# A fused S4 convolution and S2-MLP gate on one core: a new instruction order, a shorter phase step, a second staging buffer for w3 and w4, and output stores from two engines

## The chip, the core and the metric

The kernel runs on one core of one Trainium2 chip. The metric is the time of one execution on the device in microseconds (us); every time given for a kernel is the median of several executions. TensorE (PE) does matrix products and transposes, VectorE (DVE) and ScalarE (ACT) do elementwise work out of SBUF and PSUM, SyncE (SP) issues DMA transfers. Each engine runs its own list of instructions strictly in order and waits on semaphores for the others.

## The reference

The input u is 2048 rows (positions) of 512 channels. It is layer-normed to xn, which goes down two branches whose results are multiplied:

```python
xn = _layernorm(x)
s = _A_ref(xn, ...)            # S4 convolution
g = _silu(_B_ref(xn, ...))     # S2-MLP
return x + s * g

# _A_ref, per channel d with 128 states n
P = exp(dt * A * l)                        # complex, l = 0 .. 2047
K = einsum("dn,dnl,dn->dl", C, P, dt * B).real
y = irfft(rfft(xn padded) * rfft(K padded))[:2048] + xn * Dskip

# _B_ref
h  = gelu(layernorm(xn) @ w1)              # 512 x 512
hs = concat(quarters of h shifted by +1, -1, +2, -2 rows) @ w2
x1 = xn + hs
return x1 + gelu(layernorm(x1) @ w3) @ w4  # 512 x 1376, 1376 x 512
```

## The kernel before, in words

**Recorded, then ordered.** The body of `tile_mixer_kernel` (L613) does not issue instructions. Every call on an engine is recorded as an `Op` in a `Plan` (L295) with its engine, a cost, its dependences, and for ACT the function table that it needs. `Plan.order` (L406) is a list scheduler: it always takes the engine that can start earliest and, among the ops that are ready on it, the one with the lowest due value. The due values are a table of numbers, `DUE`, one for each op. `SWITCH` is added to the due value of an ACT op that needs another function table than the loaded one. Some ops (copies, affine maps, shifts) may run on ACT or on DVE (`Either`, L577); `PREFER`/`AVOID` are added to their value on the one and on the other engine. Where PE is planned to wait long, it gets "filler" matmuls of the identity into an unused bank. `Plan.issue` (L478) then emits the instructions: line L484 emits every table load, L486 every filler, L487 everything else. So nearly all rows of the profile read L487, and the names of the tiles tell the steps apart.

**The steps, in program order.** `loads` and `params` read u (into X, 128 x 16 x 512, kept in SBUF) and the state parameters, which are transposed into `par`. `token_mixing` (L1355) does the first layer norm, h = gelu(.. @ w1) (`hT`, f32 matmuls `pb<-xT,w`), writes the first stage of the Fourier transform of xn to DRAM (`u_stage1`, tiles `ue`), adds the shifted h @ w2 to X (`hs_pair`, four pairs of `pd<-w,hT` matmuls and two adds `X<-X,pd` for a group of 256 rows, the "residual stage" below), and prepares w3 and w4: `weight_squares` squares them on ACT to get a common scale, then `prep` (L1183, six calls) loads one piece of w3 and one of w4 into the staging tile `wst`, and splits each into an f16 high and low part (`w3h`, `w4h`: one affine map on ACT or DVE and one subtraction on DVE). The place of `wst` holds one piece at a time.

`tables(hf)` (L973) builds K for half hf of the channels in 8 chunks of 32 channels: `block` (L863, one for two chunks) makes the coarse phases `pab` and magnitudes (`EB`, `mag`: many small Exp on ACT), `phases` adds the coarse phases, rounds the sum (`kt<-pt`, by adding and taking away a large constant), `remainders` subtracts, `waves` takes sine and cosine on ACT, `factors` and `sums` multiply on DVE by `eg` and `mag` in seven passes over 128 x 1024, and 64 small PE matmuls for a chunk (`pc<-pt`, `pc<-kt`; 128 records in the trace) reduce over the states into `kev`, which is stored to DRAM.

`u_spectra` (L1034) does the second Fourier stage of xn for half 1 in 8 units: `uin` and `cst` are loaded, 8 matmuls `pd<-uin,cst` (16 records), two copies to `uh`, a store. `kstage1(hf)` and `products(hf)` do the same for K, multiply the spectra (`pr`) and store the inverse's first stage (`z1e`, to the DRAM scratch Zda or Zdb).

`mlp_input(g)` and `mlp(g)` (L1298, L1313) are the MLP for a group g of 256 rows: layer norm to `x1n`, a transpose, a high part (a cast) and a low part (a subtraction) `x1T`, 132 up matmuls `pb<-x1T,w3h` (f16, three products for each block, 24 for a step, 12 in the last), gelu, `ghl`, 66 down matmuls `pa<-w4h,ghl`, and two `X<-pa,wsc,X` that add the result to X. Groups go in the order `GROUPS = [1, 2, 3, 4, 5, 6, 7, 0]` (L1296).

The end: `gate(g)` puts silu on X for group g. `inverse(hf, g)` loads `zin` (scratch Zda or Zdb), does 8 small matmuls into pc or pd, and multiplies X by them (two `X<-X,pd`). `finish(g)` adds u again (`X<-X,xr`) and stores to the output in four pieces.

**What sets the order.** SP issues all DMAs in the order that the scheduler wrote, so a load that waits for its buffer holds back all the later ones. There are eight PSUM banks, in pairs a, b, c and d: `pa` takes the MLP's accumulators (and `u_stage1`), `pb` the up products, transposes and h, `pc` the K reductions, `pd` the residual stage, transposes and `u_spectra`.

The shared staging buffer and the end of the program, before:

```python
wst = Ring(early + 2 * K4, K4, 1)                     # one place
...
for g in range(8):
    gate(g)
for hf in range(2):
    for g in range(8):
        inverse(hf, g)
for g in range(8):
    finish(g)
```

Of the kernel before, what the change touches and what calls it, by code (L numbers as in the profile page):

```python
# [10 lines left out]
F32 = mybir.dt.float32  # L11
# [8 lines left out]
P = 128  # L20
# [65 lines left out]
class Op:  # L86
# [22 lines left out]
KGC = 0.93  # L109
WARM = 36  # L110
QUARTERS = 1.05

DUE = (
# [150 lines left out]
)  # L264
SWITCH = 6.17
PREFERP, AVOIDP = 3.68, -2.58
# [1173 lines left out]
```

## Time and profile before

| | us |
|---|---|
| median of 3 runs | 597.78 (596.45 to 598.2) |
| the profiled execution | 597.6 |
| its span in the trace | 595.7 |
| PE busy | 554.6 (93%) |
| DVE busy | 503.5 (85%) |
| ACT busy | 452.4 (76%) |

The profiled execution took 597.6 us on the device, of which the trace's span is 595.7; its mean granted TensorE clock was 0.959. A group in the profile is named by line, engine, operation and output <- input tiles, with the shape of both; "x" is a count. Windows give the busy time of each engine in a stretch of the span, with the granted clock (PEclk, 1.00 is full speed) and the mean busy share of the 16 DMA engines. Waits give what ended an engine's idle time. SPq and PEq are the instruction queues of SP and PE.

### The profile page before, as it was taken

The page shows a single profiled execution, that of the slowest core. Times are in us where ns is not written, and L with a number is a line of the kernel's source. Part 1 is how long each engine was busy: PE and PEld are TensorE (multiplying, and loading weights), DVE is VectorE, ACT ScalarE, POOL GpSimd, SP SyncE. Part 2 cuts the span into 40 slices and gives each one's busy share as a digit, 9 for nine tenths or more (in the row PEclk, how much of TensorE's full clock was granted, in tenths as well). Part 3 has the DMA queues.
Part 4 walks back from the last instruction along what each step waited for, and adds up shares of the span by engine and source line. Part 5 has one row for each costly group of instructions (what it writes and reads, how often), then busy time and mean ns, then how long its engine had stood idle before and what let it go on. Part 6 is the DMA issues. An engine that isn't in the chain of part 4 may idle for free.

```text
span 595.7 us, 13857 instructions
## 1 busy us (share of the span) xinstructions
PE 554.6 (93%) x5560; PEld 355.0 (60%) x5560; DVE 503.5 (85%) x816; ACT 452.4 (76%) x959; POOL 0.7 (0%) x6
## 2 busy tenths in 40 slices
PE   9879979999958799999999999999999999999962
PEld 9766647644426466556566665666755666766410
DVE  6999999999997999999999999999965256557376
ACT  3799999999998599999999999999965452113300
POOL 0000000000000000000000000000000000000000
PEclk9979989999978799999999999999999999999975
DMA  9954685212325488696333243343688688867997
GB/s 218 266 158 166 236 277 190 89 62 81 99 70 132 125 248 270 181 248 175 100 119 113 80 123 111 90 135 97 173 288 257 212 213 222 273 204 225 279 305 218
DMA packets 105232, 106.10 MB, mean 178 GB/s; under 512 B 49040, under 2 KB 83856, under 8 KB 104272
## 3 DMA queue, kind: packets, MB, share of 16 engines
q1 hardware_dynamic: 105168, 105.22, 60.8%
q8 instruction: 44, 0.72, 0.5%
q14 instruction: 20, 0.16, 0.1%
HBM read 67.45 MB, written 37.75 MB: 177 GB/s over the span
## 4 chain that ended last, share of the span: by engine, by line
PE 78%; DVE 9%; DMA 5%; ACT 4%; SPq 1%; issue 1%; DVEq 0%
PE pb L487 25%; PE pd L487 23%; PE pa L487 20%; PE pc L487 9%; DVE X L487 3%; DMA X<-in_A_u_dram 2%; DVE pt L487 2%; SPq L487 1%; DVE kt L487 1%; ACT mag L487 1%; DVE ue L487 1%; ACT L484 1%; DMA rawA<-in_A_A_re_dram 1%; DMA wst<-in_B_w_dram 1%; DMA cst<-c_gp 0%
## 5 line engine op out<-in xcount | busy, mean ns | idle before, releaser
L487 PE MATMUL pb<-x1T,w3h 128*128 128x256 f16 (+1 forms) x1056 | 127.0, 275 | 0.0
L487 PE MATMUL pa<-w4h,ghl 128*128 128x512 f16 (+1 forms) x528 | 122.9, 379 | 0.6 <-issue 0.6
L487 PEld LDWEIGHTS <-w3h 128*128 128x128 f16 (+1 forms) x1056 | 102.3, 101 | 28.8 <-issue 13.0
L484 ACT ACT_TABLE_LOAD x74 | 94.9, 1283 | 2.0 <-PEq L1428 0.7
L487 PEld LDWEIGHTS <-ghl 128*128 128x128 f16 (+1 forms) x528 | 49.6, 98 | 60.9 <-issue 9.9
L487 PE MATMUL pb<-xT,w 128*128 128x256 f32 x256 | 61.6, 393 | 1.5 <-ACT hT L487 1.4
L487 PE MATMUL pd<-w,hT 128*128 128x512 f32 x116 | 54.0, 613 | 6.2 <-DVE X L487 6.2
L487 ACT ACTIVATE mag<-par 128x64 f32<-128x64 f32 x384 | 59.3, 307 | 0.1
L487 PEld LDWEIGHTS pb<-xT,w 128*128 128x128 f32 x256 | 49.0, 197 | 13.5 <-issue 3.9
L487 DVE SCALAR_TENSOR_TENSOR ghl<-g,wsc,ghl 128x512 f16<-128x512 f32 (+1 forms) x48 | 33.5, 698 | 20.2 <-ACT ghl L487 20.2
L487 ACT ACTIVATE g<-pb,wsc 128x512 f32<-128x512 f32 (+1 forms) x48 | 30.7, 651 | 18.1 <-PE pb L487 17.4
L487 ACT ACTIVATE ghl<-g,wsc 128x512 f16<-128x512 f32 (+1 forms) x38 | 25.7, 686 | 22.7 <-PE pa L487 22.2
L487 PEld LDWEIGHTS pd<-w,hT 128*128 128x128 f32 x116 | 22.4, 196 | 32.9 <-issue 24.5
L487 DVE TENSOR_TENSOR kt<-mag,kt 128x1024 f32<-128x1024 f32 x32 | 38.9, 1215 | 0.0
L487 PE MATMUL pd<-uin,cst 128*64 128x256 f32 x256 | 34.6, 401 | 4.5 <-DMA scr_Kda<-kev 3.9
L487 DVE SCALAR_TENSOR_TENSOR pt<-kt,pt 128x2048 f32<-128x2048 f32 x16 | 36.5, 2280 | 0.0
L487 PE MATMUL pc<-pt 128*32 128x64 f32 x1024 | 31.7, 224 | 1.9 <-DVE pt L487 1.9
L487 PE MATMUL pd<-kin,cst 128*64 128x256 f32 x256 | 32.7, 387 | 0.0
L487 PE MATMUL pc<-kt 128*32 128x64 f32 x1024 | 32.0, 225 | 0.2 <-DVE ue L487 0.2
L487 ACT ACTIVATE kt<-kt,halfpi 128x2048 f32<-128x2048 f32 x16 | 31.7, 1995 | 0.1
L487 ACT ACTIVATE pt<-pt 128x2048 f32<-128x2048 f32 x16 | 30.3, 1902 | 0.1
L487 PEld LDWEIGHTS pc<-kt 128*32 128x32 f32 x1024 | 24.1, 113 | 7.8 <-issue 4.7
(156 smaller groups left out, 912.0 us busy)
## 6 DMA issues: line engine op xcount, KB each, us to landing
wst<-in_B_w_dram SPq DMA_DIRECT2D x20, 512.0 KB, 3.7
scr_Ud<-ue SPq DMA_DIRECT2D x16, 512.0 KB, 3.7
cst<-c_gp SPq DMA_DIRECT2D x24, 256.0 KB, 2.9
uin<-scr_Ud SPq DMA_DIRECT2D x16, 256.0 KB, 4.6
scr_Uh<-uh SPq DMA_DIRECT2D x8, 512.0 KB, 5.0
scr_Kfa<-k1e SPq DMA_DIRECT2D x16, 256.0 KB, 4.1
uin<-scr_Ud SPq DMA_DIRECT2D x32, 128.0 KB, 2.8
kin<-scr_Kfa SPq DMA_DIRECT2D x32, 128.0 KB, 2.9
```

The source lines that it names most:

```text
L484: self.engines["ACT"].preload_act_table_set(SETS[table])
L487: ins = [getattr(self.engines[op.eng], name)(*args, **kw).ins for name, args, kw in op.calls]
```

## The change

1. The table `DUE` is replaced, and with it the planner's constants (`SWITCH` 6.17 to 42.98, the four preferences, fixed costs for the MLP's matmul groups). The order of the instructions on every engine is another one. The line that emits ops is now L488, the table loads are L485.
2. `block` no longer rounds the coarse phases: one `tensor_scalar` and one `tensor_sub` over 128 x 768 go. The sum is still rounded in `phases`.
3. `u_spectra` stands before the first `mlp_input` in the program, uses PSUM pair a in place of d, and has its tiles in other places (class `Slots`), among them those of `vtile` and `wtile`, which hold the `x1n` of the MLP later.
4. `prep` has two staging places for w3 and w4, the second of which is where `uin` of the spectra lay.
5. Silu and inverses are recorded in the MLP's group order; the final sums go in the order 2, 3, 4, 5, 6, 7, 1, 0.
6. Output stores may be issued by SP or by ACT. In the order that results 16 are on SP and 16 on ACT, in place of 32 on SP.

```diff
+ISSUE = 0.45
+UP, DOWN = 1.345, 1.345
 DUE = (
...
-SWITCH = 6.17
-PREFERP, AVOIDP = 3.68, -2.58
-PREFER, AVOID = 1.95, 3.56
+SWITCH = 42.98
+PREFERP, AVOIDP = 72.61, -8.0
+PREFER, AVOID = 2.1, 20.89
...
+    def store(self, dst, src):
+        call = "dma_start", (dst, src), {}
+        self.plan.add({"SP": (ISSUE, call), "ACT": (ISSUE, call)}, [dst], [src], 0, dma_cost([dst, src]))
...
+    class Slots:
+        def __init__(self, places):
+            self.places, self.k = places, 0
+        def __call__(self, shape, dt, name):
+            self.k += 1
+            return at(self.places[(self.k - 1) % len(self.places)], shape, dt, name)
...
+    wst2 = Ring(early + 2 * K4, K4, 2)
...
-    usr = dict(uin=Ring(early, K4, 2), cst=Ring(early + 2 * K4, K2, 2), uh=Ring(early + 3 * K4, K4, 2))
+    usr = dict(
+        uin=Slots([early + 4 * K4, vtile.o]), uh=Slots([vtile.o + K4, wtile.o]), cst=Ring(wtile.o + K4, K2, 2),
+    )
...
-        kab = egr([P, 12 * BQ], F32, "kab")
...
-        V.tensor_scalar(kab, pab, MAGIC, -MAGIC, op0=ALU.add, op1=ALU.add)
-        V.tensor_sub(pab, pab, kab)
...
-                pu = bank[3][b].rearrange("p (a b d) -> p a b d", a=2, b=1)
+                pu = bank[0][b].rearrange("p (a b d) -> p a b d", a=2, b=1)
...
-        by_r(X2, ov[:, :, 2 * g : 2 * g + 2], to_dram=True)
+        for r in range(4):
+            E.store(ov[r][:, 2 * g : 2 * g + 2], X2[32 * r : 32 * r + 32])
...
     def prep(jp):
-        t = load_w3(jp)
+        t = load_w3(jp, wst2)
...
-        t = load_w4(jp)
+        t = load_w4(jp, wst2)
...
+    u_spectra()
     mlp_input(GROUPS[0])
-    u_spectra()
...
-    for g in range(8):
+    for g in GROUPS:
         gate(g)
     for hf in range(2):
-        for g in range(8):
+        for g in GROUPS:
             inverse(hf, g)
-    for g in range(8):
+    for g in (2, 3, 4, 5, 6, 7, 1, 0):
         finish(g)
```

Counted over the whole program, the ACT table loads are 62 in place of 74 and PE's fillers 125 in place of 57 (36 of both stand at the very start). What the new order moves is shown at three places.

**VectorE ahead of the first `x1T`,** which is the low part of the MLP's first input (the high part's cast runs on ACT). Buffer numbers are kept, since they tell the chunks of K apart. Before, the last rows ahead of it are the coarse phases of a block (`pab_265`, with the rounding `kab`), a reduction's copy `kev` and the last factors of the sixth chunk (`pt_258`):

```order
L487 TENSOR_SCALAR kab_266<-pab_265 128x768
L487 TENSOR_TENSOR kt_259<-mag_250,kt_259 128x1024
L487 TENSOR_TENSOR pab_265<-pab_265,kab_266 128x768
L487 SCALAR_TENSOR_TENSOR w3h_191<-wst_190,wsc_80,w3h_191 128x4x96
L487 TENSOR_TENSOR pab_265<-pab_265,par_93 128x256
L487 COPY kev_256<-pc1_99 128x256
L487 TENSOR_TENSOR pt_267<-par_93,ev_85 128x1024
L487 SCALAR_TENSOR_TENSOR pt_258<-mag_250,pt_258 128x1024
L487 TENSOR_TENSOR x1T_194<-pb0_96,x1T_194 128x4x128
L487 SCALAR_TENSOR_TENSOR rs_77<-mv_74,rs_77 128x2
L487 TENSOR_TENSOR pt_267<-pab_265 128x1024
L487 TENSOR_TENSOR x1T_194<-pb1_97,x1T_194 128x4x128
```

After, all eight chunks of half 0 are done by here, and the rows belong to the first chunk of half 1 (`pt_430`, `pab_429`) and to the last pieces of w3 and w4:

```order
L488 TENSOR_TENSOR pt_430<-par_93,ev_85 128x1024
L488 TENSOR_TENSOR X_91<-X_91,pd1_101 128x512
L488 BN_AGGR mv_74<-stats_73 128x2
L488 TENSOR_TENSOR pab_429<-par_93,ev_85 128x512
L488 TENSOR_TENSOR pab_429<-par_93,ev_85 128x256
L488 TENSOR_SCALAR wsc_80<-wsc_80 128x1
L488 SCALAR_TENSOR_TENSOR w3h_187<-wst_186,wsc_80,w3h_187 128x4x256
L488 TENSOR_SCALAR w4h_189<-wst_188,wsc_80 128x2x512
L488 TENSOR_TENSOR pab_429<-pab_429,par_93 128x256
L488 SCALAR_TENSOR_TENSOR w4h_189<-wst_188,wsc_80,w4h_189 128x2x512
L488 TENSOR_TENSOR x1T_218<-pb0_96,x1T_218 128x4x128
L488 TENSOR_TENSOR x1T_218<-pb1_97,x1T_218 128x4x128
```

The first `x1T` row is number 304 of the list before and number 314 after, and ahead of it stand two chunks of K and one block more, while `kab` is gone.

**PE in the residual stage** (`pd<-w,hT`), before, where the stage is followed by K reductions and `u_spectra` comes later, behind the first up matmuls:

```order
L487 MATMUL pd_100<-w_106,hT 128x512 x2
L487 MATMUL pd_100<-w_107,hT 128x512 x2
L487 MATMUL pd_101<-w_106,hT 128x512 x2
L487 MATMUL pd_101<-w_107,hT 128x512 x2
L487 MATMUL pd_100<-w_106,hT 128x512 x2
L487 MATMUL pd_100<-w_107,hT 128x512 x2
L487 MATMUL pc_98<-kt 32x64 x4
L487 MATMUL pc_98<-pt 32x64 x4
L487 MATMUL pc_98<-kt 32x64 x4
```

After, matmuls of `u_spectra` (`pa<-uin,cst`) stand between the pairs of the stage:

```order
L488 MATMUL pc_99<-pt 32x64 x4
L488 MATMUL pc_99<-kt 32x64 x4
L488 MATMUL pc_99<-pt 32x64 x4
L488 MATMUL pa_94<-uin,cst 64x256 x4
L488 MATMUL pd_101<-w_106,hT 128x512 x2
L488 MATMUL pd_101<-w_107,hT 128x512 x2
L488 MATMUL pa_95<-uin,cst 64x256 x4
L488 MATMUL pa_94<-uin,cst 64x256 x4
L488 MATMUL pd_101<-w_106,hT 128x512 x2
L488 MATMUL pd_101<-w_107,hT 128x512 x2
```

All 8 units of `u_spectra` moved ahead of the first up matmul; before, none of them was.

**VectorE around the last MLP output** (`X<-pa,wsc,X`), before. What follows it is the multiplication by the inverses' results (pc and pd) of all groups but the first:

```order
L487 TENSOR_TENSOR X_91<-X_91,pc0_98 128x256
L487 TENSOR_TENSOR X_91<-X_91,pc1_99 128x256
L487 SCALAR_TENSOR_TENSOR ghl_571<-g32_570,wsc_80,ghl_571 128x512
L487 SCALAR_TENSOR_TENSOR ghl_573<-g32_572,wsc_80,ghl_573 96x256
L487 SCALAR_TENSOR_TENSOR X_91<-pa0_94,wsc_80,X_91 128x512
L487 SCALAR_TENSOR_TENSOR X_91<-pa1_95,wsc_80,X_91 128x512
L487 TENSOR_TENSOR X_91<-X_91,pc1_99 128x256
L487 TENSOR_TENSOR X_91<-X_91,pc0_98 128x256
L487 TENSOR_TENSOR X_91<-X_91,pd1_101 128x256
L487 TENSOR_TENSOR X_91<-X_91,pd0_100 128x256
```

After, 12 further multiplications (six inverses) and one final sum with u (`xr`) have moved ahead of the last `X<-pa,wsc,X`:

```order
L488 TENSOR_TENSOR X_91<-X_91,pd0_100 128x256
L488 TENSOR_TENSOR X_91<-X_91,pd1_101 128x256 x2
L488 TENSOR_TENSOR X_91<-X_91,pd0_100 128x256
L488 SCALAR_TENSOR_TENSOR ghl_563<-g32_562,wsc_80,ghl_563 128x512
L488 SCALAR_TENSOR_TENSOR ghl_565<-g32_564,wsc_80,ghl_565 96x256
L488 TENSOR_TENSOR X_91<-X_91,pd0_100 128x256
L488 TENSOR_TENSOR X_91<-X_91,pd1_101 128x256
L488 TENSOR_TENSOR X_91<-X_91,xr_639 128x1024
L488 SCALAR_TENSOR_TENSOR X_91<-pa0_94,wsc_80,X_91 128x512
L488 SCALAR_TENSOR_TENSOR X_91<-pa1_95,wsc_80,X_91 128x512
L488 TENSOR_TENSOR X_91<-X_91,pd0_100 128x256
```

Behind the last `X<-pa,wsc,X` there are 30 multiplications by inverses and 8 sums with u before, and 18 and 7 after.

More of the change, by code (lines that the diff above doesn't have):

```diff
@@ L447, in order @@
                 cost += TABLE_LOAD
-            if e == "SP" and len(landed) >= LANES:
+            if pick.dma and len(landed) >= LANES:
                 t = max(t, landed[-LANES] + 0.1)
@@ L459, in order @@
             pick.start = t
-            if e == "SP":
+            if pick.dma:
                 chan = max(chan, t + FIRST) + pick.dma
@@ L468, in order @@
                 s.n -= 1
-                after = done + (SAME[e] if list(s.alts) == [e] else LATENCY[e] + PAD)
+                via = "SP" if pick.dma else e
+                after = done + (SAME[via] if list(s.alts) == [via] else LATENCY[via] + PAD)
                 s.ready = max(s.ready, after)
@@ L569, in call @@
             else:
-                cost = 0.45
+                cost = ISSUE
                 dma = dma_cost(aps)
@@ L1042, in u_spectra @@
             for b in range(2):
-                pu = bank[3][b].rearrange("p (a b d) -> p a b d", a=2, b=1)
+                pu = bank[0][b].rearrange("p (a b d) -> p a b d", a=2, b=1)
                 spectrum([pu[:, 0], pu[:, 1]], cst[:, b : b + 1], lambda k: uin[:, 2 * b + k], 1)
-                E.copy(uh[:, b], bank[3][b].rearrange("p (a d) -> p a d", a=2))
+                E.copy(uh[:, b], bank[0][b].rearrange("p (a d) -> p a d", a=2))
             Q.dma_start(Uh[un].rearrange("p b a d -> p (b a d)"), uh.rearrange("p b a d -> p (b a d)"))
@@ L1120, in inverse @@
             V.tensor_mul(Xh, Xh, py[a])
-    xr = []
+    xr = {}
     def finish(g):
-        if g % 2 == 0:
-            xr.append(at(xrs.pop(), [P, 4, D], F32, "xr"))
-            by_r(xr[-1], xv[:, :, 2 * g : 2 * g + 4])
+        q = g // 2
+        if q not in xr:
+            xr[q] = at(xrs.pop(), [P, 4, D], F32, "xr")
+            by_r(xr[q], xv[:, :, 4 * q : 4 * q + 4])
         X2 = X[:, 2 * g : 2 * g + 2]
-        V.tensor_add(X2, X2, xr[-1][:, 2 * (g % 2) : 2 * (g % 2) + 2])
-        by_r(X2, ov[:, :, 2 * g : 2 * g + 2], to_dram=True)
+        V.tensor_add(X2, X2, xr[q][:, 2 * (g % 2) : 2 * (g % 2) + 2])
+        for r in range(4):
+            E.store(ov[r][:, 2 * g : 2 * g + 2], X2[32 * r : 32 * r + 32])
     def pow2_scale(cols, dst_s, dst_inv, target):
@@ L1152, with load_w3, load_w4 @@
     w3t, w4t = [], []
-    def load_w3(jp):
+    def load_w3(jp, place):
         n = min(2 * P, F - jp * 2 * P)
-        t = wst([P, 4, 2 * P], F32, "wst")
+        t = place([P, 4, 2 * P], F32, "wst")
         Q.dma_start(t[:, :, :n], w3[:, jp * 2 * P : jp * 2 * P + n].rearrange("(k p) f -> p k f", p=P))
         return t[:, :, :n]
-    def load_w4(jp):
-        t = wst([P, 2, D], F32, "wst")
+    def load_w4(jp, place):
+        t = place([P, 2, D], F32, "wst")
         if jp < 5:
@@ L1169, in weight_squares @@
     def weight_squares(i):
-        t = load_w3(i) if i < 6 else load_w4(i - 6)
+        t = load_w3(i, wst) if i < 6 else load_w4(i - 6, wst)
         c = i if i < 6 else i + 2
@@ L1325, in mlp @@
                 mm = 0
-                with plan.together():
+                with plan.together(cost=UP):
                     for k in range(4):
@@ L1342, in mlp @@
                 fn = FT[j][1]
-                with plan.together():
+                with plan.together(cost=DOWN):
                     for i in range(2):
```

298 rows, old and new, of the table DUE are left out of this document.

## The prediction

> **What bounds the kernel now.** First the page's totals and its chain of work that ended last:
>
> ```profile
> PE 554.6 (93%) x5560; PEld 355.0 (60%) x5560; DVE 503.5 (85%) x816; ACT 452.4 (76%) x959; POOL 0.7 (0%) x6
> PE 78%; DVE 9%; DMA 5%; ACT 4%; SPq 1%; issue 1%; DVEq 0%
> ```
>
> PE is the bound on average, but an average hides the stages. So the second view is the busy time in six windows, cut at the first up matmul (190.8), at the end of the stall behind it (205), and at the end of the last down matmul (564.6). The two cuts on the MLP come from the row of the up matmuls here, and from the row `pa<-w4h,ghl` quoted with the tail below (558.58 + 6.65 is past 564.6 only because PE's ends are modelled: VectorE's first use of the result starts at 564.62):
>
> ```profile
> core 0: us, PE busy (x) PEld busy (x) DVE busy (x) ACT busy (x) POOL busy (x), PEclk, DMA share, GB/s
> 0.00:35.00 35.00, 29.03 (x182) 26.36 (x183) 28.57 (x80) 22.86 (x74) 0.70 (x6) 0.94 1.00 250
> 35.00:190.80 155.80, 142.72 (x1308) 89.09 (x1306) 153.13 (x247) 148.79 (x340) 0.00 (x0) 0.95 0.43 138
> 190.80:205.00 14.20, 10.32 (x67) 7.11 (x64) 10.47 (x15) 9.42 (x17) 0.00 (x0) 0.74 0.23 74
> 205.00:430.00 225.00, 223.78 (x2664) 144.85 (x2663) 217.75 (x311) 217.72 (x458) 0.00 (x0) 1.00 0.54 152
> 430.00:564.60 134.60, 134.60 (x1123) 83.95 (x1121) 71.54 (x127) 52.58 (x74) 0.00 (x0) 1.00 0.83 241
> 564.60:595.70 31.10, 14.16 (x227) 3.60 (x225) 22.03 (x40) 1.06 (x1) 0.00 (x0) 0.65 0.89 265
> ...
> L487 PE MATMUL pb<-x1T,w3h x1056: 270/273/421, 190.8 to 544.8; 128*128 128x256 f16 x160, 128*96 128x256 f16 x16
> ```
>
> Until 190.8 VectorE is full (153.13 of 155.8), ScalarE nearly (148.79), PE has 13.1 us to spare. From 205 to 564.6 PE is full, 358.4 of 359.6 us: there only PE's work counts. In the last 31.1 us VectorE is busy for 22.03 and PE for 14.16. Between 190.8 and 205 all three idle, and the clock is at 0.74. The chain of waits shows why:
>
> ```profile
> 196.52 2.58 DMA scr_Kda<-kev
> 199.09 3.66 PE pd L487 x16
> 205.31 1.88 PE pd L487 x16
> ...
> PE pd L487 <- DMA scr_Kda<-kev: 3.9, 1, 3.9
> PE pd L487 <- DVE X L487: 10.6, 7, 6.2
> ```
>
> PE stands behind the first unit of `u_spectra`, whose inputs sat in SP's queue, for 3.9 us; that unit then runs at about half pace (3.66 us for what takes 1.88 later). SP's own waits between 105 and 192 us say what held the queue:
>
> ```profile
> SPq L487 <- DMA wst<-in_B_w_dram: 28.8, 10, 4.6
> SPq L487 <- DVE w4h L487: 19.1, 5, 4.5
> SPq L487 <- DVE w3h L487: 17.3, 5, 5.0
> ```
>
> **The stage ahead of the MLP.** By the order, VectorE has 18 more passes over 128x1024 there (two more chunks), 2 more `pt<-kt,pt`, 5 more roundings or absolute values `kt<-pt`, and 4 fewer `kab` and `pab` each; ScalarE has 64 more Exp of `mag`, 15 `uh`, 4 sines or cosines, 8 `kev`, and 6 fewer table loads.
>
> ```profile
> L487 DVE TENSOR_TENSOR kt<-mag,kt 128x1024 f32<-128x1024 f32 x32 | 38.9, 1215 | 0.0
> L487 DVE SCALAR_TENSOR_TENSOR pt<-kt,pt 128x2048 f32<-128x2048 f32 x16 | 36.5, 2280 | 0.0
> L487 DVE TENSOR_SCALAR kt<-pt 128x2048 int32<-128x2048 int32 (+1 forms) x10 | 12.2, 1218 | 0.0
> L487 DVE TENSOR_SCALAR kab<-pab 128x768 f32<-128x768 f32 x8 | 4.4, 549 | 0.0
> L487 DVE TENSOR_TENSOR pab<-pab,kab 128x768 f32<-128x768 f32 x8 | 7.6, 944 | 0.0
> ...
> L487 DVE COPY ue<-pc 128x512 f32<-128x512 f32 x9 | 6.0, 683 | 0.0
> ...
> L487 ACT ACTIVATE mag<-par 128x64 f32<-128x64 f32 x384 | 59.3, 307 | 0.1
> L487 ACT COPY uh<-pd 128x512 f32<-128x512 f32 x14 | 8.0, 584 | 1.8 <-ACT rs L487 1.0 <-PE pd L487 0.7
> L487 ACT ACTIVATE kt<-kt,halfpi 128x2048 f32<-128x2048 f32 x16 | 31.7, 1995 | 0.1
> L487 ACT COPY kev<-pc 128x256 f32<-128x256 f32 x19 | 6.8, 371 | 2.1 <-PE pc L487 1.3 <-ACT kt L487 0.8
> L484 ACT ACT_TABLE_LOAD x74 | 94.9, 1283 | 2.0 <-PEq L1428 0.7
> ```
>
> VectorE: 18 x 1.215 + 2 x 2.28 + 5 x 1.218 = 32.5 added; 4 x (0.549 + 0.944) = 6.0 and 8 copies `ue` that go to ScalarE (8 x 0.683 = 5.5) taken off; some small copies and factors make it 2 us less: +19.0. ScalarE: 64 x 59.3/384 = 9.9, 15 x 0.584 = 8.8, 4 x 1.995 = 8.0, 8 x 0.371 = 3.0, the 8 `ue` about 4.7; less 6 x 1.283 = 7.7; the rest (squares of `mag` and `EB` more, two roundings fewer) about -1: +26. PE: 8 units of `u_spectra` at the 1.88 of the row at 205.31 make 15.0, and two chunks' reductions:
>
> ```profile
> 346.46 1.92 PE pc L487 x128
> ```
>
> 2 x 1.92 = 3.8, so +18.9, besides some 15 us of new fillers, which I cost at nothing as they are put where PE would wait; if a wait is shorter than was planned, part of them is paid.
>
> None of this is lost: PE's 18.9 us leave the full stretch behind, so the first up matmul may come 18.9 us later for free. How late does it come? The low part of `x1T` is on VectorE, which is full: 19 us later, less what it can take of the 2.7 us that it idles from 35 on, makes 207 to 210 for the up matmul. PE: 190.8 + 18.9 less what it can take of its 13.1 idle us is 197 to 210. ScalarE: its 26 us less what it can take of 7.0 us of idle time is 210 to 217. The latest counts, and waits between the three come on top; I take 213, with 207 to 220 as ends.
>
> The two staging buffers: by the rows of SP's waits, 36.4 us went on waiting for `w3h` and `w4h` to free the one place, each with a load behind it. VectorE did other work then, so I count nothing ahead of 190.8. Behind it, the stall of 14.2 us (3.9 idle, and about 3.4 by the clock) need not come back, since the spectra are done by then. That relief is 0 to 8 us; I take 5. Waits can also arise: an `uin` load of the spectra is in the same SP queue, behind those of `wst`, and in front of PE's list stands the residual stage. That is a rival, below.
>
> On table loads, two rows, in order of time:
>
> ```profile
> 31.58 1.28 ACT L484 ACT_TABLE_LOAD   x1
> 32.88 0.60 ACT L487 ACTIVATE hT<-pb 128x512 f32<-128x512 f32 x1
> ```
>
> The function begins 1.30 us after the load began, so a load costs 1.3 here and the 12 fewer of the whole program 15.4. The Trainium skill ("ScalarE: Activation LUTs", section "What ACT_TABLE_LOAD costs") gives a load's 1283 ns, as here, with a drain besides, about 2.7 us for a switch; by that figure the 6 loads ahead of the MLP would give 16 and not 7.7 us, and the first up matmul could come some 8 us sooner where ScalarE is last. No row here shows a drain, so my sum goes by 1.3.
>
> **From the first up matmul to the last down.** That took 564.6 - 190.8 = 373.8. Off go PE's 18.9 and the relief of 5; six more inverses stand ahead of the last down matmul, each 1.11 us in the tail at about half the clock (row below), so some 0.55 at full clock, +3. So 352.9, and the last down ends at 213 + 352.9 = 566. That is 1 us later than now: ahead of the tail I expect no gain (557 to 578 by the ends). `kab` in the second half (6 us on VectorE) and the other table loads are worth nothing here, as PE covers them: VectorE has 217.75 of 225 us, and loses the moved 19 besides. Were PE to wait, they would be the reserve.
>
> **The tail.**
>
> ```profile
> 558.58 6.65 PE L487 MATMUL pa<-w4h,ghl 128*128 128x512 f16 x30
> 564.62 1.41 DVE L487 SCALAR_TENSOR_TENSOR X<-pa,wsc,X 128x512 f32<-128x512 f32 x2 [3.51 <-PE pa L487]
> ...
> 586.74 1.23 DVE L487 TENSOR_TENSOR X<-X,xr 128x1024 f32<-128x1024 f32 x1
> 586.76 1.11 PE L487 MATMUL pc<-zin,is 64*32 64x256 f32 x16 [0.91 <-DVE X L487]
> 587.98 0.75 DVE L487 TENSOR_TENSOR X<-X,pc 128x256 f32<-128x256 f32 x2
> 588.76 1.23 DVE L487 TENSOR_TENSOR X<-X,xr 128x1024 f32<-128x1024 f32 x1
> ...
> 575.47 17.25 SPq L487 DMA_DIRECT2D out_dram<-X  x32
> ```
>
> VectorE does its 2 + 30 + 8 instructions in 22.03 us (1.41 + 30 x 0.375 + 8 x 1.23 = 22.5 by the rows), idles 3.4, and ends at 590.0; the last store lands 5.7 later. After, 12 multiplications and one sum have gone ahead of the last down matmul, where VectorE has room (71.54 of 134.6): 22.03 - 12 x 0.375 - 1.23 = 16.3. Idle time I take as 2.0 (0 to 3.4).
>
> SP issues 32 stores in 17.25 us, 0.54 each, so the last four take 2.2 of the 5.7 us; in two queues they take half, and 4.6 are left. The Trainium skill ("DMA: Bandwidth & Descriptors", section "Issuing engines are not separate DMA queues") says that issuing from several engines saves only the sequencer's time, since the same DMA engines run it all. By that rule the split is worth 1.1 us and not more, though the DMA share of 0.89 would make a second path worth more if there were one; I take 1.1 (0 to 2). On ScalarE the first two stores, which wait for a sum `X<-X,xr`, stand ahead of a table load and the last silu, and VectorE's last multiplications wait for that; but the sum comes ahead of the last `X<-pa,wsc,X` on VectorE, which the silu needs anyway, so I cost it at nothing, and at a store's issue (0.5) each if the cover is gone. The tail is 16.3 + 2.0 + 4.6 = 22.9 (20 to 26), against 31.1.
>
> **Sum.** 213 + 352.9 + 22.9 = 588.8 of span; the execution is 1.9 longer than its span (597.6 to 595.7), so 590.7, rounded to 590.5. The profiled 597.6 is within 0.2 of the median 597.78, so no correction. What a measurement tells from no change is about 0.3%, 1.8 us.
>
> **The rivals.**
>
> *The MLP starts too late (slower).* The stage ahead gets 19 to 26 us of work on three engines that are 92 to 98% full, and its end is a chain: a unit of spectra in PE's list waits for its load, that for SP's queue, that for a `w3h` on VectorE, that for `X` or for its turn; and the first `x1n` lies where the last `uh` was, so it waits for that store (2.6 us for such a store in the chain above). For it: the 6.2 us that PE waited at once for `X<-X,pd`, and SP's 36.4 us. Against: PE has 13.1 us to spare, and two staging places. The time is the first up matmul + 352.9 + 22.9 + 1.9; it equals 597.6 at 220 and decides from there: at 226 it is 604. Chance 0.18.
>
> *The tail stays (no change).* The tail is set by transfers (share 0.89, 27.7 us of 31.1), not by VectorE: 16 `zin` and 32 stores have the same bytes as before, and the `zin` of half 1 all wait for the last Zdb store. Then it keeps 31.1: 213 + 352.9 + 31.1 + 1.9 = 599, or 597 with a relief of 7. Against: stores run only from 575 on now, and VectorE's rows follow each other without a gap at the end. Chance 0.1.
>
> *More is gained.* VectorE and ScalarE run without a gap to 207, the stall is gone wholly (8), and the tail is 20: 207 + 349.9 + 20 + 1.9 = 579. For it: DVE's share of 98% shows that such packing can be had. Chance 0.12.
>
> *Forecast*, 582 to 597: chance 0.6. The range 580 to 600 leaves out the lower part of the third case and the upper part of the first, some 0.2 together. Faster: the forecast and the third rival, nearly, 0.70; same: the second and the edges, 0.11; slower 0.19.
>
> **What would show it.** The row of `pb<-x1T,w3h` should begin at 207 to 220; VectorE and ScalarE above 92% from 35 us to there. From there to the last `pa<-w4h,ghl` PE should be busy for over 98% and the stretch 348 to 358 long, with no stall of 14 us and no half clock behind the first up matmul. Behind the last `X<-pa,wsc,X` there should be some 23 us, 16 of them VectorE's, and the last store should land under 5 us after VectorE's end. A first up matmul past 220, idle time of PE on `uin` ahead of it, or a tail of 28 us or more would make the prediction wrong.

## The result, and the profile after

The changed kernel takes 582.86 us (582.08 to 583.18), against 597.72 for the kernel before, each the median of four executions: a ratio of 0.9753 with a 95% interval of 0.9735 to 0.9771, or 14.9 us less. The forecast of 590.5 had the sign, and its range of 580 to 600 held the time, but the gain is twice the 7.3 us that were forecast. The profiled execution has a span of 581.4 us.

The page's totals, after:

```profile
PE 557.4 (96%) x5696; PEld 365.0 (63%) x5696; DVE 480.6 (83%) x777; ACT 433.8 (75%) x970; POOL 0.7 (0%) x6
PE 71%; DVE 12%; DMA 9%; ACT 4%; SPq 2%; issue 1%; DVEq 0%
```

The windows of the changed kernel, cut as before at the first up matmul (211.6) and at VectorE's first use of the last MLP output (560.2), with the columns of the prediction's table:

```profile
0.00:35.00 35.00, 31.30 (x246) 30.93 (x247) 25.86 (x69) 22.32 (x86) 0.70 (x6) 0.95 0.99 222
35.00:211.60 176.60, 168.49 (x1763) 107.86 (x1764) 174.91 (x266) 170.65 (x424) 0.00 (x0) 0.99 0.59 185
211.60:225.00 13.40, 13.40 (x115) 9.05 (x121) 13.24 (x30) 13.31 (x17) 0.00 (x0) 1.00 0.70 165
225.00:430.00 205.00, 205.00 (x2394) 132.58 (x2379) 184.56 (x281) 177.81 (x377) 0.00 (x0) 1.00 0.50 145
430.00:560.20 130.20, 130.20 (x1046) 81.42 (x1043) 66.12 (x109) 47.34 (x67) 0.00 (x0) 1.00 0.77 224
560.20:581.40 21.20, 8.98 (x147) 3.17 (x145) 15.92 (x27) 2.34 (x2) 0.00 (x0) 0.61 0.69 214
```

Three things stand out. Between 35 us and the first up matmul VectorE is busy for 174.91 of 176.6 us, and PE's clock is 0.99 in place of 0.95. From there to 560.2 PE is busy without a gap, at full clock: the stall of 14.2 us behind the first up matmul is gone. The tail is 21.2 us long, 15.92 of them VectorE's.

The two cuts can be found in every trace, from the first row `pb<-x1T,w3h` and the last pair of rows `X<-pa,wsc,X`, so all runs are compared by the same three terms (us of the profiled span):

| | first up matmul | from there to the last MLP output | tail | span |
|---|---|---|---|---|
| before | 190.8 | 373.8 | 31.1 | 595.7 |
| forecast | 213 | 352.9 | 22.9 | 588.8 |
| after | 211.6 | 348.6 | 21.2 | 581.4 |
| kab_back | 219.9 | 360.0 | 21.4 | 601.3 |
| kab_fixed | 222.5 | 354.2 | 21.2 | 597.9 |
| kab_order | 212.2 | 354.4 | 21.3 | 587.9 |
| no_fillers | 215.1 | 348.7 | 20.9 | 584.7 |
| one_staging | 213.7 | 380.8 | 21.3 | 615.8 |
| spectra_late | 191.0 | 401.5 | 53.4 | 645.9 |
| sp_stores | 212.1 | 348.8 | 22.9 | 583.8 |
| inverses_late | 212.2 | 346.2 | 26.6 | 585.0 |
| pool_sums | 211.1 | 348.7 | 22.6 | 582.4 |
| before_no_kab | 190.0 | 375.8 | 32.6 | 598.4 |
| before_two | 190.2 | 370.0 | 31.9 | 592.1 |
| before_two_no_kab | 190.0 | 371.6 | 32.2 | 593.8 |

All three terms came out below the forecast, by 1.4, 4.3 and 1.7 us. Each row is one execution, and the runs come from several chips, so a difference of a microsecond between two rows is not a finding: where the order ahead of it was that of the changed kernel and nothing was added, the first up matmul came between 211.1 and 212.2. Two of kab_fixed's twelve executions, of 693 and 2679 us, were slow ones and are not in its ratio.

### The profile page after: what moved, and what is told of

It is laid out like the page before. It is cut to its first block, busy times and chain, and to the rows that moved or that the text cites. A ratio compares the mean times of both kernels' runs of the same rounds, so it can differ in the third digit from the quotient of the medians.

```text
span 581.4 us, 14100 instructions
## 1 busy us (share of the span) xinstructions
PE 557.4 (96%) x5696; PEld 365.0 (63%) x5696; DVE 480.6 (83%) x777; ACT 433.8 (75%) x970; POOL 0.7 (0%) x6
## 4 chain that ended last, share of the span: by engine, by line
PE 71%; DVE 12%; DMA 9%; ACT 4%; SPq 2%; issue 1%; DVEq 0%
PE pb L488 24%; PE pa L488 20%; PE pd L488 19%; PE pc L488 8%; DVE pt L488 4%; DMA X<-in_A_u_dram 4%; DVE X L488 3%; DVE kt L488 2%; SPq L488 2%; DMA wst<-in_B_w_dram 1%; DMA zin<-scr_Zdb 1%; DMA ld<-in_A_log_dt_dram 1%; DMA scr_Zdb<-z1e 1%; ACT ue L488 1%; ACT kt L488 1%
## 5 line engine op out<-in xcount | busy, mean ns | idle before, releaser
L488 PE MATMUL pb<-x1T,w3h 128*128 128x256 f16 (+1 forms) x1056 | 124.1, 273 | 0.0
L488 PE MATMUL pa<-w4h,ghl 128*128 128x512 f16 (+1 forms) x528 | 121.9, 380 | 0.0
L488 PEld LDWEIGHTS <-w3h 128*128 128x128 f16 (+1 forms) x1056 | 101.4, 100 | 26.6 <-issue 13.6
L488 PEld LDWEIGHTS <-ghl 128*128 128x128 f16 (+1 forms) x528 | 49.7, 98 | 61.2 <-issue 8.9
L488 PE MATMUL pb<-xT,w 128*128 128x256 f32 x256 | 61.3, 393 | 5.0 <-ACT hT L488 5.0
L488 ACT ACTIVATE mag<-par 128x64 f32<-128x64 f32 x384 | 59.7, 310 | 2.1 <-DVE tm L488 1.2
L488 PEld LDWEIGHTS pb<-xT,w 128*128 128x128 f32 x256 | 48.5, 195 | 17.6 <-ACT hT L488 6.5
L488 ACT ACTIVATE g<-pb,wsc 128x512 f32<-128x512 f32 (+1 forms) x48 | 30.7, 650 | 37.6 <-PE pb L488 37.4
L488 DVE SCALAR_TENSOR_TENSOR ghl<-g,wsc,ghl 128x512 f16<-128x512 f32 (+1 forms) x48 | 33.3, 698 | 26.4 <-ACT ghl L488 26.3
L488 PE MATMUL pd<-w,hT 128*128 128x512 f32 x116 | 53.7, 603 | 0.5 <-DVE X L488 0.4
L488 ACT ACTIVATE ghl<-g,wsc 128x512 f16<-128x512 f32 (+1 forms) x34 | 23.4, 692 | 27.6 <-PE pa L488 27.1
L488 DVE TENSOR_TENSOR kt<-mag,kt 128x1024 f32<-128x1024 f32 x32 | 38.7, 1213 | 0.0
L488 PEld LDWEIGHTS pd<-w,hT 128*128 128x128 f32 x116 | 21.0, 190 | 26.1 <-issue 24.6
L488 DVE SCALAR_TENSOR_TENSOR pt<-kt,pt 128x2048 f32<-128x2048 f32 x16 | 36.4, 2277 | 0.0
L488 PE MATMUL pd<-kin,cst 128*64 128x256 f32 x256 | 32.7, 387 | 0.0
L488 ACT ACTIVATE kt<-kt,halfpi 128x2048 f32<-128x2048 f32 x16 | 31.9, 1997 | 0.1
L488 PE MATMUL pc<-kt 128*32 128x64 f32 x1024 | 30.6, 221 | 1.0 <-DVE kt L488 0.9
L488 DVE TENSOR_TENSOR pr<-pd,uin 128x512 f32<-128x512 f32 x32 | 20.4, 685 | 13.2 <-PE pd L488 12.5
L488 ACT ACTIVATE pt<-pt 128x2048 f32<-128x2048 f32 x16 | 30.7, 1920 | 0.1
L488 PE MATMUL pc<-pt 128*32 128x64 f32 x1024 | 30.1, 219 | 0.0
L488 PEld LDWEIGHTS pc<-kt 128*32 128x32 f32 x1024 | 23.5, 110 | 9.4 <-issue 6.8
```

What stands on the lines that cost most here:

```text
L488: ins = [getattr(self.engines[op.eng], name)(*args, **kw).ins for name, args, kw in op.calls]
```

## The experiments

Ratios are to the kernel before, timed on the same chip; the changed kernel's own is 0.9753. A difference "by the ratios" is that of two ratios times 597.7 us.

**The coarse rounding put back (kab_back).** Every block gets two 128x768 passes again. Their due value and planned cost are those of the addition that they stand with.

```diff
-        V.tensor_add(pb, pb, phr[:, qs].unsqueeze(2).to_broadcast([P, BQ, 4]))
+        ph = phr[:, qs].unsqueeze(2).to_broadcast([P, BQ, 4])
+        with plan.together(cost=dve_cost("tensor_add", (pb, pb, ph))):
+            V.tensor_scalar(pab, pab, 1.0, 0.0, op0=ALU.mult, op1=ALU.add)
+            V.tensor_tensor(pab, pab, pab, op=ALU.max)
+            V.tensor_add(pb, pb, ph)
```

> The changed kernel with the two 128x768 passes of a block put back on VectorE as work of the same cost that changes no value (a multiplication by 1, a maximum of the tile with itself); the planned order ahead of the MLP stays. Theory A (three stages: VectorE sets the first up matmul, PE all from there to the last down matmul, VectorE the tail): five blocks lie ahead of the first up matmul, 5 x (0.549 + 0.944) = 7.5 us, so the first up matmul and the end move by 6 to 7.5 us, and the three blocks behind it cost nothing. Theory B (VectorE's total counts wherever it is freed): 8 blocks, +12 us. Theory C (staging and transfers set the stage ahead of the MLP): the first up matmul stays within 1.5 us.

It took 603.44 us, ratio 1.0076 (1.0052 to 1.01): 0.8% slower than the kernel before. The first up matmul came 8.3 us later, a little more than the 6 to 7.5 of theory A, but the stretch behind it also grew, by 11.4 us, which none of the theories expected. In that stretch the planner had written another order. So the next two runs hold the order fixed.

**The same work in the changed kernel's own order (kab_fixed).** The order of all operations, the engine of each and the fillers are written out as a list (`kept`). The extra passes lie over 512 and 256 columns, behind the product for `pa` and the sum for `pb`, some 1.8 us for a block.

```diff
+        return kept
...
+    def again(t):
+        plan.ops[-1].alts["DVE"][1] += [
+            ("tensor_scalar", (t, t, 1.0, 0.0), {"op0": ALU.mult, "op1": ALU.add}),
+            ("tensor_tensor", (t, t, t), {"op": ALU.max}),
+        ]
...
+        again(pab[:, : 8 * BQ])
...
+        again(pab[:, 8 * BQ :])
```

> The changed kernel with its own order of instructions written out and kept, in which each of the 8 blocks has the cost of the coarse rounding back on VectorE (a multiplication by 1 and a maximum with itself, over 512 and over 256 columns: about 1.8 us for a block). Theory A (VectorE's work delays the first up matmul one for one, and PE covers it behind): five blocks ahead, 8 to 9 us, first up matmul at 219 to 221, the stretch to the last down matmul at 349 to 351: +8 to +10 us in all. Theory B (the 20 us that the same work cost in the planner's own new order are its effect on the kernel wherever it lies): the stretch grows to 355 or more, +15 us or more.

599.05 us, ratio 0.9994 (0.9974 to 1.0013): the whole gain is gone. The distance to the changed kernel's ratio is 2.4%, 14.4 us, for 8 x 1.8 = 14.6 us of added work. In the profiles the first up matmul is 10.9 us later, for 9.1 us of work ahead of it, and the stretch behind it is 5.6 us longer, for 5.5 us of work in it; the two make 16.5 us, more than the 14.4 by the ratios, but the profiles are single executions on different chips (kab_order, on this run's chip, has its first up matmul at 212.2, 10.3 us ahead of this one). The windows of this run (the second ends 0.7 us behind the table's cut), and what PE waited for behind the first up matmul:

```profile
35.00:222.50 187.50, 172.16 (x1764) 109.40 (x1762) 183.64 (x288) 172.93 (x429) 0.00 (x0) 0.97 0.54 170
222.50:577.40 354.90, 350.12 (x3552) 223.46 (x3560) 270.86 (x432) 238.57 (x458) 0.00 (x0) 1.00 0.61 173
```

```profile
PE pb L645 <- DVE x1T L645: 1.7, 3, 0.7
PE pc L645 <- ACT kev L645: 1.3, 1, 1.3
PE pd L645 <- DVE pr L645: 0.8, 1, 0.8
PE pa L645 <- DVE ghl L645: 0.7, 1, 0.7
```

PE is no longer full there (350.12 of 354.9), and what it waits for are many small things that VectorE delivers too late. VectorE has 84 us to spare in that stretch by its busy time, but not at the places where the order needs it. Theory A is near ahead of the first up matmul (222.5 for 219 to 221) and fails behind it; there theory B is near (354.2 for 355 or more, +14.4 for +15 or more).

**The order alone (kab_order).** The changed kernel without the rounding, in the order that the planner wrote for kab_back, again from a list.

```diff
+        return kept
```

> The changed kernel, without the coarse rounding, in the order that the planner wrote when its work was put back (kab_back). Theory A (the 11 us that kab_back lost between the first up and the last down matmul came of its order there): first up matmul at 211 to 213, the stretch at 357 to 361, 8 to 12 us more than the changed kernel. Theory B (they came of the work itself): the stretch at 349 to 351, within 2 us of the changed kernel.

589.94 us, ratio 0.9851 (0.9822 to 0.988), 5.9 us more than the changed kernel by the ratios: between the two theories. The first up matmul is where it was (212.2), the stretch is 354.4. So of the 11.4 us that kab_back lost there, 5.8 came of its order and the other 5.6 of the work, as much as kab_fixed shows for the work.

**The rounding taken out of the kernel before (before_no_kab).** The order is that of the kernel before, row for row; the two passes are cut to one column, which leaves the first rounding of the coarse phases out.

```diff
+        for o in plan.ops[-2:]:
+            name, args, kw = o.alts["DVE"][1][0]
+            o.alts["DVE"][1][0] = name, tuple(a[:, :1] if is_ap(a) else a for a in args), kw
```

> The kernel before in its own order, with the two 128x768 passes of a block cut to 128x1 (their effect on the sum is left out). Theory A (VectorE sets the first up matmul, PE what follows): four blocks' passes lie ahead, 4 x 1.39 = 5.6 us; the first up matmul comes 4 to 5.6 us earlier and the end as much. Theory B (VectorE's total): -10 to -12 us. Theory C (staging sets that stage): within 1 us.

599.48 us, ratio 1.002 (0.9994 to 1.0046): nothing. The first up matmul moved by 0.8 us, though VectorE, 98% busy before, had 5.1 us less to do ahead of it (176.61 us busy for 181.70). The chain of waits from 35 to 190 us, of the kernel before and then of this run, by share:

```profile
by line: PE pd L487 34.7%; PE pb L487 17.4%; PE pc L487 7.0%; DVE pt L487 6.1%; DVE kt L487 5.5%; DVE ue L487 4.6%; DMA wst<-in_B_w_dram 3.6%; issue 3.3%; ACT L484 2.4%; ACT mag L487 2.4%; PE pa L487 1.9%; DVE eg L487 1.5%; DVE X L487 1.5%;
```

```profile
by line: PE pd L487 34.6%; PE pb L487 20.8%; PE pc L487 6.7%; ACT L484 4.7%; PE pa L487 3.4%; DMA wst<-in_B_w_dram 3.4%; DMA scr_Ud<-ue 2.9%; issue 2.6%; DVE pt L487 2.5%; ACT mag L487 2.4%; DVE ue L487 1.9%; ACT wst L487 1.6%; ACT xT L487 
```

Before, over half of the chain is PE's f32 products for h and the residual stage (`pb`, `pd`), and VectorE's phases (`pt`, `kt`) have 12%. Without the rounding, VectorE's share falls and PE's stays. Above all, of the 149 pieces of the first chain none is one of the rounding's rows (`kab<-pab`, `pab<-pab,kab`): they stood beside the chain, and taking them away shortened nothing. None of the three theories had this as its reason; theory C has the number, for another reason. In the changed kernel PE's share is also the largest, but there the rows of `pab` lie on the chain, and the passes added in kab_fixed lengthened it. The changed kernel up to 212 us, then kab_fixed up to 222 us:

```profile
by line: PE pd L488 26.7%; DVE pt L488 13.3%; PE pb L488 9.9%; PE pa L488 9.0%; DVE kt L488 7.2%; DMA X<-in_A_u_dram 6.3%; PE pc L488 3.5%; issue 3.4%; ACT ue L488 2.5%; ACT kt L488 2.2%; ACT L485 2.1%; DVE pab L488 1.9%; DVE eg L488 1.9%; 
```

```profile
by line: PE pd L645 22.2%; DVE pt L645 12.8%; PE pb L645 8.7%; DVE kt L645 8.6%; DVE pab L645 7.1%; PE pa L645 5.7%; issue 4.3%; PE pc L645 4.1%; DVE stats L645 2.6%; DVE X L645 2.5%; ACT kt L645 2.1%; ACT ue L645 1.4%; ACT L642 1.3%; DVE w
```

`pab` goes from 1.9% of 177 us to 7.1% of 187, from 3.4 to 13.3 us, which is most of the 10.9.

**Two staging places in the kernel before (before_two, before_two_no_kab).** The order is again that of the kernel before.

```diff
+    wst2 = Ring(early + 2 * K4, K4, 2)
...
-        t = load_w3(jp)
+        t = load_w3(jp, wst2)
...
-        t = load_w4(jp)
+        t = load_w4(jp, wst2)
```

> The kernel before, its order written out and kept, with two staging places for the pieces of w3 and w4. Theory A (the stall behind the first up matmul came of loads queued behind those of w3 and w4, which waited for the one place): the first up matmul within 2 us, the wait of PE of 3.9 us and the half clock behind it gone, -3 to -8 us. Theory B (the stage ahead is one coupled chain through PE, and the spectra's place is what ended the stall): within 1.5 us.

594.14 us, ratio 0.9922 (0.9897 to 0.9947): 4.7 us less. SP's waits between 105 and 192 us, where the kernel before had 28.8 us on the staged loads, now 2.7 (those on `w3h` and `w4h` did not shrink, 39.6 for 36.4):

```profile
SPq L645 <- ACT kev L645: 27.0, 5, 10.6
SPq L645 <- DVE w3h L645: 20.3, 4, 8.2
SPq L645 <- DVE w4h L645: 19.3, 3, 7.7
SPq L645 <- PE pb L645: 3.2, 1, 3.2
SPq L645 <- DMA wst<-in_B_w_dram: 2.7, 2, 2.4
```

The window behind the first up matmul has its clock back, and PE works for 11.49 of 14.8 us in place of 10.32 of 14.2:

```profile
190.20:205.00 14.80, 11.49 (x104) 8.18 (x96) 12.73 (x18) 12.23 (x26) 0.00 (x0) 1.00 0.55 167
```

PE's wait of 3.9 us is gone from that window, but others have come into it, of which this is the longest:

```profile
PE pd L645 <- ACT uh L645: 1.7, 1, 1.7
```

So the 3.9 us and the slow clock came of the loads queued behind the one staging place, as theory A has it, but most of what was won is the clock: from the first up matmul to the last MLP output PE is busy for 365.9 us in place of 368.7, and idles for 4.2 in place of 5.1. With the rounding's passes cut as well:

> The kernel before, its order kept, with both: two staging places, and the two passes of a block cut to 128x1. Theory A (each part hides the other: with the loads early and VectorE relieved, the first up matmul comes earlier): 5 to 10 us less than the kernel before. Theory B (coupled chain through PE's residual stage, which neither shortens): within 2 us of before_two.

594.6 us, ratio 0.9921 (0.9893 to 0.9949): the same as before_two. In this order taking the rounding's work off VectorE wins nothing, with or without the second place: theory B.

**One staging place in the changed kernel (one_staging).**

```diff
-        t = load_w3(jp, wst2)
+        t = load_w3(jp, wst)
...
-        t = load_w4(jp, wst2)
+        t = load_w4(jp, wst)
```

> The changed kernel with one staging place for the pieces of w3 and w4; the planner moves some rows for it (5 us more VectorE work ahead of the first up matmul, by another split of the last residual groups). Theory A (VectorE is full there whatever is loaded when): the first up matmul 3 to 6 us later, of which PE gives back what moved ahead of it, so 0 to +4 us. Theory C (staging sets that stage): +6 us or more, with waits of VectorE on the loads.

618.85 us, ratio 1.0358 (1.0308 to 1.0409). The first up matmul is only 2.1 us later, and nearly all of the loss is behind it, 32 us: PE idles for 22 of them, in many small pieces. The number is in the range of theory C, but VectorE waited for no staged load ahead of the first up matmul, so its reason is not borne out. **The spectra late (spectra_late)** went the same way:

> The changed kernel with the spectra of xn behind the first MLP input again, in the places, banks and due values that they had before (raised by 20); the planner then also moves other work: ahead of the first up matmul stand 26 us less of VectorE's and 25 us less of ScalarE's work and 30 us less of PE's, and behind the last MLP output 32 multiplications and 8 sums. Theory A (each stage by its engine): first up matmul at about 186 to 190, from there to the last down matmul 349 + 30 + 0 to 8 of stall = 379 to 387, tail 32: 597 to 607 of span, 16 to 26 us more. Theory B (where the spectra stand is neutral, as they only fill gaps of PE): within 4 us.

647.9 us, ratio 1.0846 (1.0798 to 1.0894), with the first up matmul at 191.0, near theory A's number, but 401.5 and 53.4 for the other two terms, out of both theories. In both runs the planner wrote a new order with due values that belonged to another program, and kab_order shows what that alone can cost. They say little of the staging place or of the spectra.

**The fillers (no_fillers).**

```diff
-            for _ in range(op.fill):
+            for _ in range(0):
```

> The changed kernel without its 89 filler matmuls behind the first 36, nearly all of them in the first 12 us. Theory A (VectorE sets the first up matmul, PE has 8 us to spare there): within 1 us. Theory B (the fillers keep the granted clock up, 0.99 in place of 0.95 between 35 us and the first up matmul, and that is where part of the gain comes from): the clock falls to 0.95 there and the time grows by 3 to 6 us.

586.93 us, ratio 0.9802 (0.9775 to 0.983): 2.9 us more by the ratios, with the first up matmul 3.5 us later (3 us against sp_stores and inverses_late, timed on the same chip) and the rest as it was. The 89 fillers lie between 11 and 37 us in the trace, not in the first 12 as the expectation says. Two windows and the products for h, first of the changed kernel, then of this one:

```profile
24.00:35.00 11.00, 10.96 (x99) 10.78 (x98) 10.99 (x42) 9.50 (x32) 0.00 (x0) 1.00 1.06 233
35.00:45.00 10.00, 9.72 (x81) 6.97 (x82) 9.42 (x36) 9.60 (x19) 0.00 (x0) 1.00 0.90 254
...
L488 PE MATMUL pb<-xT,w x256: 378/380/635, 39.9 to 148.6; 128*128 128x256 f32 x128
```

```profile
24.00:35.00 11.00, 1.08 (x4) 0.71 (x4) 10.99 (x41) 9.51 (x29) 0.00 (x0) 0.50 1.04 245
35.00:45.00 10.00, 8.26 (x41) 5.50 (x42) 10.00 (x39) 8.30 (x18) 0.00 (x0) 0.56 0.58 159
...
L488 PE MATMUL pb<-xT,w x256: 379/379/794, 42.6 to 151.1; 128*128 128x256 f32 x128
```

Without fillers the granted clock is at half from 24 us on and still is when the first useful products come; the first product for h is 2.7 of the 3.5 us late (42.6 for 39.9). From 35 us to the first up matmul the clock is 0.97, not 0.95 as theory B expected; the size is near B's.

**The tail (sp_stores, inverses_late, pool_sums).** The stores on SP alone:

```diff
-        self.plan.add({"SP": (ISSUE, call), "ACT": (ISSUE, call)}, [dst], [src], 0, dma_cost([dst, src]))
+        self.plan.add({"SP": (ISSUE, call)}, [dst], [src], 0, dma_cost([dst, src]))
```

> The changed kernel with all 32 output stores issued by SP. Theory A (issue only: the last four stores queue behind each other at 0.54 us each): +0.5 to +1.5 us, the first up matmul and the last down matmul as they are. Theory B (a second path of transfers is what shortened the tail): +3 us or more. Theory C (VectorE alone sets the tail): within 0.3 us.

584.7 us, ratio 0.9767 (0.9741 to 0.9792): the tail is 1.7 us longer in the profile, all of it behind VectorE's end, and 0.8 by the ratios, which their intervals can't tell from nothing. Theory B is out; the profile speaks for theory A, and the ratios do not exclude C. The inverses behind the MLP:

```diff
+        if hf or g != GROUPS[0]:
+            for o in plan.ops[-3:]:
+                o.vt += 400
```

> The changed kernel with due values raised for all inverses but the first, so that 26 multiplications and 8 sums in place of 18 and 7 stand behind the last MLP output on VectorE. Theory A (VectorE sets the tail): the tail grows by 8 x 0.375 + 1.23 = 4.2 us, the last down matmul comes some 2 us earlier by the inverses' matmuls: +2 to +4 us. Theory B (the tail is set by the round trip of the inverse's first stage through DRAM, from the last products on): within 0.5 us.

586.35 us, ratio 0.9793 (0.9768 to 0.9817), +2.4 by the ratios, whose intervals just touch: the tail 5.4 us longer, the last MLP output 1.8 us earlier. Theory A. Three of the final sums on GpSimd:

```diff
+    ON_POOL = (3, 5, 7)
...
-        V.tensor_add(X2, X2, xr[q][:, 2 * (g % 2) : 2 * (g % 2) + 2])
+        (G if g in ON_POOL else V).tensor_add(X2, X2, xr[q][:, 2 * (g % 2) : 2 * (g % 2) + 2])
```

> The changed kernel with three of the eight final sums with u on GpSimd in place of VectorE. Theory A (VectorE sets the tail): 3 x 1.23 = 3.7 us less on VectorE behind the last MLP output; if GpSimd takes under 3 us for one beside VectorE, -2 to -3.7 us. Theory B (the tail is set by transfers): within 0.5 us. If GpSimd is slower than 4 us for one or holds VectorE up: +1 to +5 us.

584.42 us, ratio 0.9781 (0.974 to 0.9823): no gain, the tail is 1.4 us longer. GpSimd's sums, and then some of VectorE's in the same stretch:

```profile
562.83 4.68 POOL L488 TENSOR_TENSOR X<-X,xr 128x1024 f32<-128x1024 f32 x2 [561.53 <-DMA out_dram<-X]
569.49 2.35 POOL L488 TENSOR_TENSOR X<-X,xr 128x1024 f32<-128x1024 f32 x1 [1.98 <-DVE X L488]
```

```profile
563.87 0.75 DVE L488 TENSOR_TENSOR X<-X,pc 128x256 f32<-128x256 f32 x2
...
566.21 2.39 DVE L488 TENSOR_TENSOR X<-X,xr 128x1024 f32<-128x1024 f32 x1
568.52 0.74 DVE L488 TENSOR_TENSOR X<-X,pd 128x256 f32<-128x256 f32 x2
569.96 2.96 DVE L488 TENSOR_TENSOR X<-X,xr 128x1024 f32<-128x1024 f32 x1
```

While GpSimd adds, VectorE's own sum takes 2.39 and 2.96 us in place of 1.23. GpSimd's three cost VectorE 2.9 us and saved it 3.7, and VectorE waited for PE's inverses besides (1.6 us idle from 559.8 to its end, for 0.2 in the changed kernel), so that its part of the tail is 17.1 us long in place of 16.1. Neither theory A nor B; the last sentence of the expectation, GpSimd holding VectorE up, is what came.

## Why the prediction was right in sign and half in size

**The step that failed.** The way the gain is made was forecast rightly: a later first up matmul paid for by PE's moved work, no stall behind it, a shorter tail. What failed is the size of the terms that the prediction could not read from rows and put at a middle of their ranges, and the largest of these is the relief from the stall: put at 5, it measured 8.0. The tail's idle time was put at 2.0 and measured 0.2, and the first up matmul, taken at 213, came at 211.6. With 1.3 us less in the rest of the stretch these make up nearly all of the 7.4 us by which the span of 588.8 was missed.

**The first up matmul (213 forecast, 211.6).** VectorE's added work was right to a tenth: 181.70 us busy up to it before (the first two windows of the prediction: 28.57 + 153.13), 200.77 after (the first two windows above: 25.86 + 174.91), so +19.1 for a forecast of +19.0. ScalarE's was sized too high: 171.65 to 192.97, +21.3 for +26. But neither ended last. VectorE's row of `x1T` ended at 210.4, and PE, busy for 61.47 of the 61.6 us from 150 on, went from the residual stage straight into the first up matmul:

```profile
210.70 1.02 PE L488 MATMUL pd<-w,hT 128*128 128x512 f32 x2
211.56 4.64 PE L488 MATMUL pb<-x1T,w3h 128*128 128x256 f16 x41
```

PE had 25.8 us more to do from 35 us on (168.49 for 142.72), not 18.9. The prediction overlooked that the products for h, which began at 39.9 us after the change, had begun ahead of 35 us before it:

```profile
20.48 7.43 PE L487 MATMUL pb<-xT,w 128*128 128x256 f32 x32
```

That 213 is so near is in part luck: it was taken from ScalarE's range of 210 to 217, with PE's at 197 to 210. The fillers were costed at nothing; they won some 3 us here, most of them by 43 us.

"VectorE is full" was read from 98% busy time, and that alone does not say what its work is worth. In the kernel before, 5.1 us less of it moved the first up matmul by 0.8. In the changed kernel, 9.1 us more moved it by 10.9: there VectorE idled for only 1.7 of 176.6 us, so at least 7.4 had to show. The two are not the same test, since one takes work away and the other adds it; what parts them is whether the rows lie on the chain of waits. What work taken off VectorE would win in the changed kernel was not run.

**From there to the last MLP output (352.9 forecast, 348.6).** It was -18.9 for moved work, -5 of relief, +3 for inverses. PE idled for 5.1 us in this stretch before (368.70 busy of 373.8) and for none after. The half pace cost 2.9 us: 3.66 in place of 1.88 for the unit of spectra, by the prediction's rows, and 2.56 in place of 1.42 for the 12 up matmuls behind it, by two rows of the kernel before:

```profile
202.75 2.56 PE pb L487 x12
212.27 1.42 PE pb L487 x12
```

That makes a relief of 8.0, the top of the stated range of 0 to 8. The other two terms held: the units of spectra moved at 1.88 us each and the chunks' reductions at 1.92, and PE's rows with `zin`, the inverses, are busy for 4.17 us in the stretch after and 1.33 before, +2.8 for +3. With the relief at 8.0 the sum is 373.8 - 18.9 - 8.0 + 3 = 349.9; the 1.3 us from there to 348.6 are not assigned. Two staging places alone win 4.7 us by the ratio in the old order, most of it the half pace; in the new order the spectra have left the stretch as well, and no run parts the two.

**"Worth nothing here, as PE covers them"**, said of the rounding in the second half, is refuted by kab_fixed for the order of the changed kernel: 5.5 us of work there cost 5.6. It did not change the sum, since PE is full after, as forecast; but it hid how little room there was. With the rounding in it, PE would not have been full.

**The tail (22.9 forecast, 21.2).** VectorE's work was right (15.92 for 16.3). VectorE's last rows:

```profile
560.18 1.41 DVE L488 SCALAR_TENSOR_TENSOR X<-pa,wsc,X 128x512 f32<-128x512 f32 x2
...
575.07 1.23 DVE L488 TENSOR_TENSOR X<-X,xr 128x1024 f32<-128x1024 f32 x1
```

From 560.2 to 576.3 it idles for 0.2 us, where 2.0 were put in; from its end to the end of the span it is 5.1 us, for 4.6 and for "under 5". The second path of stores is worth 0.8 to 1.7 us, for a forecast of 1.1. By the rule of the Trainium skill that was weighed there ("DMA: Bandwidth & Descriptors", section "Issuing engines are not separate DMA queues") no more was to be had, and the runs agree.

**The rivals.** "The MLP starts too late" did not come, but its point of decision, 220, was near: kab_fixed, with the first up matmul at 222.5, is no faster than the kernel before. "The tail stays" fell (21.2 for 31.1). "More is gained" (579) was nearer to the result than the forecast; it got 0.12 because the middle of an unknown was taken three times: the stall, the idle time, the waits. For the stall the order that was read had removed the cause, as the spectra stood ahead of it and the loads had two places.

**What the change is worth by its parts.** The shorter phases gain nothing in the old order: 1.002 (0.9994 to 1.0046). The new order with the rounding's work in it is no faster either: 0.9994, with 1.8 us for a block where the real passes took 1.5; scaled by 1.5/1.8, the rounding is worth some 12 of the 14.9 us in the new order, an estimate, which leaves some 3 for all the rest. Both together: 0.9753. That holds for an order that was written without the rounding; what the planner could reach with due values made for it is not known. What the second staging place and the place of the spectra are worth in the new order stays open, as no run undid one of them with the order held.

## What to carry to other kernels

Busy time, even 98% of a stage, does not say what taking work from an engine wins. Look whether the rows that will go lie on the chain of waits through the stage, and take them away in a run with the order unchanged. In a schedule that is packed from a table of due values, work that comes on top can cost its full length, even beside an engine that is full. Undoing a part through the planner measures a new, unfitted order as well (5.8 of 11.4 us here); write the order out and hold it. Where the changed order removes the cause of an unknown cost, take that end of its range and not the middle.

## What the runs showed of the hardware

A sum of two 128x1024 f32 tiles on VectorE took 1.23 us, and 2.39 and 2.96 us while GpSimd ran one of its own (2.35 us each); multiplications with one input in PSUM kept their 0.37 us (0.75 for two at 563.87, beside GpSimd's). Both slow sums ended 1.1 us behind GpSimd's (568.60 behind 567.51, 572.92 behind 571.84), nearly their own 1.23, as if they had hardly moved while GpSimd's ran; spans on GpSimd are rough. The Trainium skill ("GPSIMD Engine Reference", section "1. Specifications") names such contention for VectorE instructions with two SBUF inputs, and this trace agrees. And 89 matmuls that compute nothing, nearly all in the first 36 us, brought a matmul at 211 us forward by 3 to 3.5 us, with the granted clock from 24 to 35 us at 1.00 in place of 0.50.
